# Attention and a token MLP on one core: half of the query projections moved into the attention loop, the second half's outputs moved behind it

## The chip, the core and the metric

The kernel runs on one core of a Trainium2 chip. The core has TensorE (PE in the profile, with PEld for its weight loads), VectorE (DVE), ScalarE (ACT), GpSimd (POOL) and SyncE (SP), which here issues nearly all transfers. The engines run their own instruction streams in order and wait for one another through semaphores. The metric is the device time of one execution in microseconds (us), as the median of several runs. The kernel before takes 1286.77 us, the median of 3 runs from 1286.64 to 1287.14.

## The reference

The input x has 2048 rows (tokens) and 512 columns. Two results are mixed by a gate of each row:

```python
x = A_x
g = _sigmoid((x * gate_w).sum(-1, keepdims=True))
a = _A_ref(x, A_wqkv, A_wo)           # softmax attention, 32 heads of 16 columns, then @ wo
b = _B_ref(x, B_w1, B_b1, B_w2, B_b2) # layernorm, then over the tokens: w1 (2048 x 1792), gelu, w2 (1792 x 2048)
return g * a + (1 - g) * b
```

In `_A_ref`, qkv = x @ wqkv, scores = q k^T / 4 for each head, p = softmax(scores), o = p v, and the result is o @ wo. All is in float32.

## The kernel before, in words

**Splitting.** Where float32 accuracy is wanted, a matrix is split into a part `hi`, rounded to the short form fp32r that PE multiplies at full speed, and the rest `lo`; a product is then three: hi x hi, hi x lo, lo x hi (`split` L64, `products` L69). A 128-column block of a product with 512 inner elements is so 4 x 3 = 12 matmuls of 128x512.

**Stages.** (1) x is loaded in 16 tiles of 128 rows, transposed on PE into `xt_hi`, `xt_lo` (L185 to L194), and v = x wv is put out by `v_out` (L221) into one SBUF tile `v`, with a column of ones beside each head, which later gives the softmax's sums. (2) The q/k stage (L362 to L387): for each block b of 128 columns (8 heads), four pieces of 512 tokens of k and four of q, each through `project` (12 matmuls into one of eight PSUM banks) and `parts` (L352: ACT casts hi, DVE subtracts lo, for queries ACT also makes |q| times the greatest |k|, a third plane; SP stores the planes `pc`, of which there are three buffers, to `kp_d` and `qp_d` in device memory). `greatest` keeps the largest |k| and |q|; from these `bring_most` and `least_shifts` set a flag that chooses the general path after the end, which these inputs do not take. (3) Layer one of the MLP (L449 to L475) with its gelu into `u_hi`, `u_lo`. (4) The attention loop, with layer two beside it. (5) The end, from L986.

**The attention loop.** There are 2 halves of the queries (1024 each) x 16 pairs of heads = 32 groups, each with 4 phases: 128 phases. `load_k` and `load_q` (L510, L515) fetch the next group's stacks from device memory: three planes of keys and four of queries for each of the two heads. Four rows of a stack's 64 x 2 are no data but -1 or the third plane, whose product shifts the exponent; the -1 rows of keys are set once by a POOL memset (`shift_rows` L491). In a phase, PE makes 16 scores of 128x512 (L917), ACT takes the exponential of 12 straight from PSUM, DVE copies the other four to SBUF (L934) for one ACT instruction of 2048 columns (L949), and `apply_v` (L792) makes 64 small products with v, whose sum DVE adds to `ot` (L821).

**Dense products beside the scores.** A score has only 64 inner rows, so it uses half of PE's rows; the other half takes half of a *dense* matmul at the same time (L926). A dense matmul is so done in two phases, its upper 64 rows in the one, its lower 64 in the next. Two phases are a *slot*, and there are 64 slots with at most 14 dense matmuls. The dictionary `dense` says what each slot holds, `calls` what is issued at a phase's start (transfers above all), `later` what DVE does at its end. They all sum into one PSUM bank, `dn`, and the slot's last step reads it out. Before, the first 28 matmuls of layer two are done at full width ahead of the loop (`first`, L831 to L837); slots 0 to 45 hold the rest of layer two (16 tiles of 42 matmuls), 46 and 47 nothing, 48 to 55 the output projections of the first half's eight token tiles (12 matmuls each), 56 to 63 the first 6 or 9 of the 12 of the second half's. The attention result is divided by its sums when it is fetched back from device memory (`fetch_half`, `fetch_o`, `load_wq`), into SBUF places of layer two, which is over by then (`open_end`).

**The end.** `others` (L995) makes the products that are left of the second half's eight output tiles, `last_pair` those with the last pair of heads, whose sums are only just known, and `finish` adds them to the MLP's share and stores them.

**What sets the order.** In stages 2 and 3 a scheduler orders the instructions of each engine; in the loop and at the end (`tc.manual_schedule`) they stand in the order of the code. Pools with `reuse_waits` make a new tile wait for the last reader of the old one.

## Time and profile before

| what | value |
|---|---|
| median of 3 runs | 1286.77 us |
| profiled execution | 1287.07 us, of which the span of instructions is 1284.9 us |
| PE / ACT / DVE / POOL busy | 1272.5 / 1087.6 / 670.8 / 199.1 us |
| mean granted clock of TensorE | 0.998 |
| stage 1 to first q/k product | 0 to 57.5 us |
| q/k stage, layer one | to 144.6, to 296.7 us |
| attention loop: first score, last product with v | 304.6, 1265.4 us |
| last product of the end | 1277.7 us |

A matmul's row in the trace gives its duration through the pipeline (0.39 us for 128x512), while the next begins 0.23 us after it; so PE's rate is read from starts, not from durations. In the chain of waits each row is a piece of work and the time that passed with it. Stretches are given as from:to, then length, then busy time and (x) count for PE, PEld, DVE, ACT and POOL, then granted clock, share of the transfer engines and GB/s. In rows of instructions the first number is the start, the second the time to the end of the group.

### The profile page before, as it was taken

The numbers are of one execution on the slowest core, as the hardware profiler recorded it, in microseconds if no ns is written. First come the engines' busy times: TensorE is split into PE (matmuls) and PEld (weight loads), VectorE is DVE, ScalarE is ACT, GpSimd is POOL, SyncE is SP. The second block draws the span as 40 slices with busy tenths as digits, with TensorE's granted clock in tenths as the row PEclk, the third lists the DMA queues.
The fourth block names the chain that finished last, engine by engine and source line by source line (L and its number), as shares of the span: only waits on it lengthen the run. The fifth ranks groups of instructions, "written<-read, shape, count | busy, mean of one in ns | idle before, by whom it ended". The sixth has DMA issues, their size and how long they took to land.

```text
span 1284.9 us, 33049 instructions
## 1 busy us (share of the span) xinstructions
PE 1272.5 (99%) x13281; PEld 837.1 (65%) x13281; DVE 670.8 (52%) x1138; ACT 1087.6 (85%) x1537; POOL 199.1 (15%) x306
## 2 busy tenths in 40 slices
PE   9999999999999999999999999999999999999997
PEld 7888888886666666666666666666666565655554
DVE  5675362537444544544444444444444675645555
ACT  3443343437999999999999999999999999999994
POOL 0210244455111111111111111111110000000000
PEclk9999999999999999999999999999999999999999
DMA  4496643327343344343334434433433754344412
GB/s 132 140 319 270 230 124 99 95 78 164 67 88 76 68 90 85 71 80 81 77 61 91 84 67 84 81 75 59 82 64 60 174 140 115 82 91 102 81 38 80
DMA packets 93581, 133.19 MB, mean 104 GB/s; under 512 B 16277, under 2 KB 55339, under 8 KB 90348
## 3 DMA queue, kind: packets, MB, share of 16 engines
q1 hardware_dynamic: 92844, 129.94, 41.8%
q8 instruction: 107, 1.75, 0.6%
q10 hardware_dynamic: 576, 1.05, 0.2%
q14 instruction: 54, 0.44, 0.1%
HBM read 97.00 MB, written 33.93 MB: 102 GB/s over the span
## 4 chain that ended last, share of the span: by engine, by line
PE 94%; ACT 4%; issue 1%; DVE 0%; DMA 0%; SPq 0%; ACTq 0%
PE av L799 29%; PE s L917 23%; PE t L917 12%; PE acc L417 12%; PE acc L74 10%; PE s L799 5%; PE dn L926 2%; ACT p L879 1%; ACT p L938 1%; ACT pe L949 1%; PE pa L1000 1%; PE dn L835 1%; PE acc L188 1%; PE acc L255 0%; PE pa L1030 0%
## 5 line engine op out<-in xcount | busy, mean ns | idle before, releaser
L938 ACT ACTIVATE p<-s 128x512 f32<-128x512 f32 x768 | 416.9, 817 | 1.5 <-PE s L917 1.5
L879 ACT ACTIVATE p<-t 128x1024 f32<-128x1024 f32 x352 | 370.5, 1300 | 0.0
L917 PE MATMUL s<-qs,ks 64*128 64x512 f32 x1344 | 342.0, 403 | 0.2
L934 DVE COPY pe<-s 128x512 f32<-128x512 f32 x512 | 318.0, 684 | 6.3 <-PE s L917 5.8
L917 PEld LDWEIGHTS s<-qs,ks 64*128 64x128 f32 x1344 | 234.7, 184 | 99.7 <-issue 52.2
L821 DVE TENSOR_TENSOR ot<-av,ot 128x512 f32<-128x512 f32 (+2 forms) x137 | 83.5, 610 | 393.3 <-PE av L799 393.0
L799 PE MATMUL av<-p,v 128*32 128x256 f32 x4904 | 288.1, 379 | 0.0
L949 ACT ACTIVATE pe<-pe 128x2048 f32<-128x2048 f32 x129 | 280.9, 2181 | 0.0
L799 PEld LDWEIGHTS av<-p,v 128*32 128x32 f32 x4904 | 159.3, 110 | 105.3 <-issue 0.2
L917 PE MATMUL t<-qs,ks 64*128 64x512 f32 x704 | 179.9, 450 | 1.7
L926 PE MATMUL dn<-u_hi,w_lo 64*128 64x512 f32 x430 | 174.8, 407 | 0.0
L926 PE MATMUL dn<-u_lo,w_hi 64*128 64x512 f32 x430 | 174.8, 406 | 0.0
L926 PE MATMUL dn<-u_hi,w_hi 64*128 64x512 f32 x428 | 173.5, 405 | 0.0
L67 POOL TENSOR_TENSOR w_lo<-w_raw,w_hi 128x512 fp32r<-128x512 f32 (+1 forms) x126 | 149.3, 1191 | 124.6 <-ACT w_hi L66 108.1
L917 PEld LDWEIGHTS t<-qs,ks 64*128 64x128 f32 x704 | 87.8, 184 | 90.0 <-ACT p L938 89.8
L930 POOL MEMSET token<- 1x1 f32 x124 | 12.3, 100 | 822.7 <-PE dn L926 757.4
L799 PE MATMUL av<-pe,v 128*32 128x256 f32 x2048 | 137.2, 385 | 0.1
L66 ACT CAST w_hi<-w_raw 128x512 fp32r<-128x512 f32 (+1 forms) x67 | 38.1, 569 | 79.4 <-PE acc L417 58.8
L799 PEld LDWEIGHTS av<-pe,v 128*32 128x32 f32 x2048 | 53.4, 109 | 54.8 <-ACT p L938 32.2
L417 PE MATMUL acc<-h_hi,w_hi 128*128 128x512 f32 x224 | 87.1, 389 | 0.0
L417 PE MATMUL acc<-h_lo,w_hi 128*128 128x512 f32 x224 | 87.1, 389 | 0.0
L417 PE MATMUL acc<-h_hi,w_lo 128*128 128x512 f32 x224 | 87.1, 389 | 0.0
(150 smaller groups left out, 1517.4 us busy)
## 6 DMA issues: line engine op xcount, KB each, us to landing
w_raw<-in_B_w_dram SPq DMA_DIRECT2D x96, 256.0 KB
ks<-kp SPq DMA_DIRECT2D x192, 128.0 KB
qs<-qp SPq DMA_DIRECT2D x256, 64.0 KB
qp<-pc SPq DMA_DIRECT2D x16, 768.0 KB
x<-in_A_x_dram SPq DMA_DIRECT2D x32, 256.0 KB
kp<-pc SPq DMA_DIRECT2D x16, 512.0 KB
w_raw<-in_B_w_dram SPq DMA_DIRECT2D x32, 128.0 KB
bp<-row SPq DMA_DIRECT2D x16, 256.0 KB
```

Of the source, the lines that this page charges most:

```text
L66: copy(hi, src)
L67: return sub(lo, src, hi.bitcast(F32), ALU.subtract)
L74: nc.tensor.matmul(ps, a, b, start=start and n == 0, stop=stop and n == last)
L417: nc.tensor.matmul(p, a, b, start=first and k == 0, stop=last and k == 2)
L799: mm = nc.tensor.matmul(av[32 * j : 32 * (j + 1), i * QC : (i + 1) * QC], v_flat[:, v_at : v_at + 32], pt[:, h * QC : (h + 1) * QC], start ...
L821: nc.vector.tensor_tensor(x, y, x, ALU.add)
L879: nc.scalar.activation(pt, twos[low, low + 1], AF.Exp, scale=SCALE)
L917: nc.tensor.matmul(s, kt[grp][rows_i, c * P : (c + 1) * P], qt[grp][rows_i, qb * NB : (qb + 1) * NB], start=True, stop=True,)
L926: mm = nc.tensor.matmul(ps, a[half], b[half], start=begin and not second, stop=last and bool(second))
L934: nc.vector.tensor_copy(pt, s)
L938: nc.scalar.activation(pt, s, AF.Exp, scale=SCALE)
L949: nc.scalar.activation(x, x, AF.Exp, scale=SCALE)
```

## The change: what it does

The q/k stage projects all four pieces of k but only the first two of q in each block (`jobs`). The other two of each block, eight pieces of 12 matmuls, become dense slots of the attention loop (`late_query`): after each of layer two's first eight tiles comes one such slot. For that the second half of transposed x is stored to device memory (`xt_d`, four transfers of 1 MB during block 0) and loaded again in two steps (`load_xt`), and the query weights are stored and loaded for each slot (`wq_d`). A slot's result goes through five DVE operations and three stores into `qp_d[1]`, which the second half's groups read. The bound check moves with it, from layer one into the loop.

Layer two then starts in slot 0 and nothing is done at full width ahead of the loop. Slots 0 to 31 hold eight tiles of layer two and the eight query pieces, 32 to 55 the other eight tiles, 56 to 63 the outputs of the first half. All 96 matmuls of the second half's outputs stand in the end.

v is four tiles, one for each block of eight heads. When a block's last group is over, its place takes fetched rows of the first half (`fetch_left`), later others. v itself is first stored to device memory for the general path.

The first place is PE between layer one (`acc`) and the first scores (`s`, from the stacks `qs`, `ks`). Before:

```order
L417 MATMUL acc<-h_lo,w_hi 128x512
L417 MATMUL acc<-h_hi,w_lo 128x512
L835 MATMUL dn<-u_hi,w_hi 128x512
L835 MATMUL dn<-u_lo,w_hi 128x512
L835 MATMUL dn<-u_hi,w_lo 128x512
```

and, 23 rows of L835 further on,

```order
L835 MATMUL dn<-u_hi,w_hi 128x512
L917 MATMUL s_2818<-qs,ks_2703 128x512
L926 MATMUL dn<-u_lo,w_hi 128x512
L917 MATMUL s_2819<-qs,ks_2703 128x512
L926 MATMUL dn<-u_hi,w_lo 128x512
```

Now, at the same place:

```order
L417 MATMUL acc<-h_lo,w_hi 128x512
L417 MATMUL acc<-h_hi,w_lo 128x512
L982 MATMUL s_2692<-qs,ks_2619 128x512
L991 MATMUL dn<-u_hi,w_hi 128x512
L982 MATMUL s_2693<-qs,ks_2619 128x512
L991 MATMUL dn<-u_lo,w_hi 128x512
L982 MATMUL s_2691<-qs,ks_2619 128x512
L991 MATMUL dn<-u_hi,w_lo 128x512
```

The 28 full-width products are gone, and the first score follows layer one's last product. On POOL the memset of the first keys' shift rows stands, before and now, behind the same last weight split; before:

```order
L67 TENSOR_TENSOR w_lo<-w_raw,w_hi 128x512 x3
L493 MEMSET ks_2703 16x2048 x2
L930 MEMSET token 1x1
L493 MEMSET ks_2704 16x2048 x2
```

and now:

```order
L67 TENSOR_TENSOR w_lo<-w_raw,w_hi 128x512 x3
L489 MEMSET ks_2619 16x2048 x2
L995 MEMSET token 1x1
L489 MEMSET ks_2620 16x2048 x2
```

Nothing moved there. The second place is DVE at the end of slot 3 (the fourth phase of the second group): `pe` are the copied scores, `dn` the dense bank, `row` a buffer of 128x512, `z` the greatest values. Before:

```order
L934 COPY pe<-s_3645 128x512
L934 COPY pe<-s_3676 128x512
L523 TENSOR_SCALAR row<-dn,b2x_75,omg 128x512
L66 CAST w_hi<-w_raw 128x512
L821 TENSOR_TENSOR ot<-av,ot 128x512
```

Now:

```order
L999 COPY pe<-s_3515 128x512
L999 COPY pe<-s_3546 128x512
L66 CAST row<-dn 128x512
L67 TENSOR_TENSOR row<-dn,row 128x512
L564 TENSOR_SCALAR row<-dn,most 128x512
L565 SCALAR_TENSOR_TENSOR row<-row 128x512
L566 TENSOR_REDUCE z<-dn 128x1
L894 TENSOR_TENSOR ot<-av,ot 128x512
```

Five operations stand now between the last copy and the addition to `ot`, four of which read `dn`. The third place is SP's queue at the change from stage 1 to the q/k stage. Before:

```order
L173 DMA x<-in_A_x_dram 128x512 x3
L159 DMA wc_raw<-in_A_wqkv_dram 128x4x128 x2
L135 DMA w_raw<-in_B_w_dram 128x512 x4
```

with two more of each of the last two kinds, and then the first `kp` store. Now:

```order
L400 DMA xt_68<-xt_hi 512x1x512
L183 DMA x<-in_A_x_dram 128x512
L400 DMA xt_69<-xt_lo 512x1x512
L183 DMA x<-in_A_x_dram 128x512
L169 DMA wc_raw<-in_A_wqkv_dram 128x4x128 x2
L145 DMA w_raw<-in_B_w_dram 128x512 x2
L397 DMA wq_72<-wc_hi 128x512
L169 DMA wc_raw<-in_A_wqkv_dram 128x4x128
L400 DMA xt_70<-xt_hi 512x1x512
L400 DMA xt_71<-xt_lo 512x1x512
L397 DMA wq_73<-wc_lo 128x512
```

The four stores of transposed x and the first query weights (`wq`) have come in ahead of the first key store. The diff, cut to its core:

```diff
-    qp_d = [dram.tile([3, P, S], F32, name=f"qp{b}") for b in range(ND)]
+    qp_d = [[dram.tile([3, P, S // 2], F32, name=f"qp{h}{b}") for b in range(ND)] for h in range(2)]
+    xt_d = {n: [dram.tile([P, ND, NB], F32, name=f"xt{n}{i}") for i in range(2)] for n in (2, 3)}
+    wq_d = [[dram.tile([P, ND, P], F32, name=f"wq{b}{i}") for i in range(2)] for b in range(ND)]
+    v_d = [dram.tile([P, NS * (P // DH) * VC], F32, name=f"v{b}") for b in range(ND)]
...
-    v_pool = ctx.enter_context(tc.tile_pool(name="v", bufs=1))
-    v_flat = v_pool.tile([P, NS * H * VC + HALF], F32, name="v")
-    v = v_flat[:, : NS * H * VC].rearrange("p (t h c) -> p t h c", h=H, c=VC)
+    v_pool = ctx.enter_context(tc.tile_pool(name="v", bufs=1, reuse_waits="tile"))
+    BH = P // DH
+    BV = NS * BH * VC
+    def v_tile(b, dtype):
+        return v_pool.tile([P, BV + DH], dtype, name=f"v{b}")
+    vb = [v_tile(b, F32) for b in range(ND)]
+    v = [x[:, :BV].rearrange("p (t h c) -> p t h c", h=BH, c=VC) for x in vb]
...
-            nc.scalar.copy(v[:, t, :, 0:DH], ps.rearrange("p (h d) -> p h d", d=DH))
+            heads = ps.rearrange("p (b h d) -> p b h d", h=BH, d=DH)
+            for b in range(ND):
+                nc.scalar.copy(v[b][:, t, :, 0:DH], heads[:, b])
...
+        jobs = [(n, True) for n in range(NQ)] + [(n, False) for n in range(NQ // 2)]
         for b in range(ND):
             wk_b, wq_b = qk_w.pop(0), qk_w.pop(0)
             kmax = bd.tile([P, NQ], F32, name="kmax")
-            qmax = bd.tile([P, NQ], F32, name="qmax")
-            for n in range(NQ):
-                ps = project(wk_b, n)
-                parts(ps, kp_d[b], n)
-                greatest(kmax[:, n : n + 1], ps)
-            nc.vector.tensor_reduce(kmax[:, 0:1], kmax, axis=AX.X, op=ALU.max)
-            nc.vector.tensor_scalar_mul(kmax[:, 0:1], kmax[:, 0:1], BOUND_SLACK)
-            for n in range(NQ):
-                ps = project(wq_b, n)
-                parts(ps, qp_d[b], n, kmax[:, 0:1])
-                greatest(qmax[:, n : n + 1], ps)
-                if n % 2 and qk_cols:
+            for at, (n, keys) in enumerate(jobs):
+                ps = project(wk_b if keys else wq_b, n)
+                if keys:
+                    parts(ps, kp_d[b], n)
+                    greatest(kmax[:, n : n + 1], ps)
+                else:
+                    parts(ps, qp_d[0][b], n, most[:, b : b + 1])
+                    greatest(qmax[:, b, n : n + 1], ps)
+                if n == NQ - 1:
+                    nc.vector.tensor_reduce(kmax[:, 0:1], kmax, axis=AX.X, op=ALU.max)
+                    nc.vector.tensor_scalar_mul(most[:, b : b + 1], kmax[:, 0:1], BOUND_SLACK)
+                if at in (1, 4) and qk_cols:
                     qk_w.append(wcols(qk_cols.pop(0)))
-                if n % 2 == 0:
-                    c = 2 * b + n // 2
+                if at in (2, 5):
+                    c = 2 * b + at // 3
                     ln_load(ln, c)
                     ln_rows(ln, c)
-                if b == ND - 1:
+                if at in (3, 4):
+                    nc.sync.dma_start(wq_d[b][at - 3], wq_b[at - 3].bitcast(F32))
+                if b == 0 and keys:
+                    src = (xt_hi, xt_lo)[n % 2][:, :, (2 + n // 2) * NB : (3 + n // 2) * NB]
+                    nc.sync.dma_start(xt_d[2 + n // 2][n % 2], src.bitcast(F32))
+                if b == ND - 1 and at > 1:
                     load_weight()
-                    if n > 0:
+                    if at > 2:
                         split_weight()
-            nc.vector.tensor_reduce(qmax[:, 0:1], qmax, axis=AX.X, op=ALU.max)
-            nc.vector.tensor_mul(most[:, b : b + 1], qmax[:, 0:1], kmax[:, 0:1])
...
-                    if f0 == 0 and c == 0:
-                        bring_most()
-                    if f0 == 0 and c == NH + 4:
-                        least_shifts()
...
+    def load_xt(n):
+        xt[n] = [o_pool.tile([P, ND, NB], F32R, name=f"big{i}") for i in range(2)]
+        for dst, src in zip(xt[n], xt_d[n]):
+            nc.sync.dma_start(dst.bitcast(F32), src)
...
+    def late_query(b, n):
+        box = []
+        def load():
+            for i in range(2):
+                t = out_pool.tile([P, D], F32, name="row", bufs=3)
+                nc.sync.dma_start(t.rearrange("p (k c) -> p k c", k=ND), wq_d[b][i])
+                box.append(t.bitcast(F32R).rearrange("p (k c) -> p k c", k=ND))
+        def out():
+            ps, cols = box[2], slice((n - 2) * NB, (n - 1) * NB)
+            hi, lo, most_k = (out_pool.tile([P, D], F32, name="row", bufs=3) for _ in range(3))
+            split(hi.bitcast(F32R), lo.bitcast(F32R), ps, nc.vector.tensor_copy, nc.vector.tensor_tensor)
+            nc.vector.tensor_scalar(most_k, ps, most[:, b : b + 1], None, ALU.mult)
+            nc.vector.scalar_tensor_tensor(most_k.bitcast(F32R), most_k, -1.0, most_k, ALU.mult, ALU.max)
+            nc.vector.tensor_reduce(qmax[:, b, n : n + 1], ps, axis=AX.X, op=ALU.max, apply_absolute_value=True)
+            for i, t in enumerate((hi, lo, most_k)):
+                nc.sync.dma_start(qp_d[1][b][i, :, cols], t)
+        def step(k, j):
+            first, last = k == j == 0, k == ND - 1 and j == 2
+            if first:
+                box.append(ps_dn.tile([P, D], F32, name="dn"))
+            a, x = ((0, 0), (0, 1), (1, 0))[j]
+            return box[2], box[a][:, k, :], xt[n][x][:, k, :], first, last, out if last else None
+        return [(step, k, j) for k in range(ND) for j in range(3)], load
...
+    def v_block(b):
+        if b not in in_place_of_v:
+            in_place_of_v[b] = v_tile(b, F32R)[:, : NS * P].rearrange("p (t x) -> p t x", x=P)
+        return in_place_of_v[b]
...
+    def fetch_left(k, *ats):
+        first = 8 * (k % 2)
+        parts = [v_block(k // 2)[:, at : at + 4] for at in (first, first + 4)]
+        fetch(0, k, left, parts, out_pool.tile([P, NB], F32, name="row", bufs=3), ats)
+    def fetch_right(k, *ats):
+        both = pieces(place(k))
+        fetch(0, k, right, (both[:, :4], both[:, 4:]), end.tile([P, QW], F32, name="o_sum", bufs=3)[:, :NB], ats)
...
-    for k in range(ND):
-        call(6 * k + 5, load_wo, k, 6 * k + 5)
-    steps = second_layer(0)
-    first, at = steps[:28], put(steps[28:], 0, [14])
-    for t in range(1, NS):
+    call(1, load_xt, 2)
+    for b in range(ND):
+        call(6 + b, nc.sync.dma_start, v_d[b], vb[b][:, :BV])
+    at, queries = 0, [(b, n) for n in (2, 3) for b in range(ND)]
+    for t in range(NS):
         at = put(second_layer(t), at, [14] * 3)
+        if queries:
+            b, n = queries.pop(0)
+            at = put_whole(late_query(b, n), at)
+            if (b, n) == (ND - 1, 2):
+                call(2 * at, load_xt, 3)
+            if (b, n) == (ND - 1, 3):
+                call(2 * at, open_wo)
+                on_dve(2 * at + 1, greatest_of_all)
+                call(2 * at + 2, bring_most)
+                on_dve(2 * at + 4, least_shifts)
+                for k in range(ND):
+                    call(2 * at + 5 + 4 * k, load_wo, k, 2 * at + 5 + 4 * k)
...
+    left, right = slice(0, NB), slice(NB, QW)
+    for k in range(ND):
+        p0 = PHASES * (NP + 4 * (k // 2 + 1)) + 3 + 4 * (k % 2)
+        assert p0 + 3 < 2 * at
+        call(p0, fetch_left, k, p0 + 2, p0 + 2, p0 + 2)
...
-        call(p0 + k // 2, fetch_half, k, left, p0 + 2 + k // 2, p0 + 2 + k // 2)
-        call(p0 + 2 + k // 2, fetch_half, k, right, p0 + 5 + k, p0 + 5 + k)
-    at += 2
+        call(p0 + k, fetch_right, k, p0 + k + 2, p0 + k + 2, p0 + k + 2)
     for t in range(NH):
-        at = put_output(t, 3 * ND, at)
-    p1 = PHASES * (NP + 2 * 4) + 3
-    call(p1, fetch_o, 1, 0, (8, 9), (p1 + 2, p1 + 3, p1 + 3))
-    call(p1 + 4, fetch_o, 1, 1, (10, 11), (p1 + 6, p1 + 7, p1 + 7))
-    p2 = PHASES * (NP + 3 * 4) + 3
-    assert p2 >= 2 * at - 1
-    call(p2, fetch_o, 1, 2, (0, 1), (p2 + 1, p2 + 1, p2 + 2))
-    call(p2 + 4, load_wq, p2 + 4)
-    call(LAST - 1, fetch_o, 1, 3, (2, 3), (LAST, LAST, LAST), 3)
-    for t in range(NH, NS):
-        at = put_output(t, 6 if 2 * at < p2 + 3 else 9, at)
-    assert at == NG * PHASES // 2
+        at = put_whole(project(t), at)
+        call(p0 + 2 * t, load_base, NH + t)
+    assert p0 + 7 < 2 * (at - 4) and at == NG * PHASES // 2
+    call(p0 + 4, fetch_o, 0, p0 + 6, p0 + 6, p0 + 7)
+    call(p0 + 6, fetch_o, 1, p0 + 8, p0 + 8, p0 + 10)
+    call(p0 + 7, load_wq, p0 + 7)
+    call(p0 + 9, fetch_o, 2, p0 + 11, p0 + 12, p0 + 12)
+    call(LAST - 1, lambda: fetch_o(3, LAST, LAST, LAST, pairs=3))
...
-        for n, (step, *args) in enumerate(first):
-            if n and n % 12 == 0:
-                split_weight(nc.vector.tensor_copy, nc.vector.tensor_tensor)
-            ps, a, b, start, stop, done = step(*args)
-            nc.tensor.matmul(ps, a, b, start=start, stop=stop)
-            if done:
-                done()
...
-        LATE = 3, 5, 7
+        LATE = 3, 5, 6, 7
         def others(*tiles, m=0, n=3 * ND):
             for t in tiles:
-                mms = list(enumerate(o_matmuls(1, NH + t, early[NH + t], 3 * ND)))
+                mms = list(enumerate(o_matmuls(1, NH + t, 0, 3 * ND)))
...
-        others(2, 4, 6)
+        others(2, 4)
...
-        last_pair(0, parts)
-        others(1)
+        last_pair(0, parts, LATE)
+        others(6, 1)
...
-        others(*LATE)
+        others(3, 5, 7)
```

143 lines of the change are left out of this document (75 added, 68 removed).

## The prediction

> **What bounds the kernel now.** I read the page first (span, busy shares, slices, chain), then the chain of waits in order of time, then stretches with the busy time of each engine, and last single instructions at the places that the change touches.
>
> ```profile
> span 1284.9 us, 33049 instructions
> PE   9999999999999999999999999999999999999997
> ACT  3443343437999999999999999999999999999994
> PE 94%; ACT 4%; issue 1%; DVE 0%; DMA 0%; SPq 0%; ACTq 0%
> ```
>
> TensorE (PE) is busy throughout, and ScalarE (ACT) from the tenth slice (about 300 us) to the last but one. So there are two regimes: PE alone before 300 us, both of them in the attention loop. The chain gives the stretches:
>
> ```profile
> 52.04 92.54 PE acc L74 x408
> 144.58 149.39 PE acc L417 x660
> 298.05 6.63 PE dn L835 x28
> 945.40 3.65 PE av L799 x64
> 975.39 3.65 PE av L799 x64
> 1035.34 3.65 PE av L799 x64
> 1065.34 3.64 PE av L799 x64
> ```
>
> The 408 products of L74 (24 of the last two v tiles, then 32 x 12 = 384 of the q and k projections) run without a gap at 92.54 / 408 = 0.2268 us each. Layer one follows, then the 28 products of `first`, then attention. The last four rows stand at the same place of four groups: 945.40 to 975.39 is a group whose slots hold 14 dense products (30.0 us), 975.39 to 1035.34 two groups, one of them with two empty slots (59.95, so 29.97 each), 1035.34 to 1065.34 a group with 12 (30.0). A phase takes 7.49 us whatever rides beside its scores. Why:
>
> ```profile
> 975.00:1005.00 30.00, 29.90 (x352) 16.62 (x350) 13.75 (x22) 30.00 (x43) 0.80 (x4) 1.00 0.41 94
> 1035.00:1065.00 30.00, 29.82 (x370) 18.06 (x370) 22.20 (x39) 30.00 (x43) 0.88 (x5) 1.00 0.51 125
> 985.15 2.19 ACT L949 ACTIVATE pe<-pe 128x2048 f32<-128x2048 f32 x1
> 992.62 2.20 ACT L949 ACTIVATE pe<-pe 128x2048 f32<-128x2048 f32 x1
> ```
>
> Columns of the first two rows are PE, weight loads, DVE, ACT, POOL, clock, DMA share, GB/s. ACT is busy 30.00 of 30.00 with and without dense products, and its exponentials return every 7.47 us also in empty slots. The attention loop belongs to ACT; products of 12 to 14 per slot are free there as long as nothing else waits on them.
>
> **The change part by part.** The sum is made against the profiled execution, 1287.07 us (span 1284.9 and 2.2 around it); the median of the runs shown is 0.30 lower, 1286.77.
>
> *Fewer projections ahead.* Two of four query pieces in each of four blocks leave the q/k stage: 2 x 4 x 12 = 96 products x 0.2268 = **-21.8 us**, if PE still sets the pace. With them go 8 ACT casts, 8 ACT multiples, 8 DVE subtractions and 8 reductions, all beside PE. What is added there are transfers on SP's queue: four of 1 MB (transposed x) and eight of 0.26 MB (query weights), while eight of 0.79 MB go.
>
> ```profile
> 57.50:144.60 87.10, 87.10 (x386) 72.13 (x385) 56.16 (x111) 36.93 (x63) 6.90 (x5) 1.00 0.71 260
> 65.00:110.00 45.00, 45.00 (x201) 37.24 (x200) 31.98 (x59) 21.17 (x37) 5.60 (x4) 1.00 0.89 317
> 60.00:65.00 5.00, 5.00 (x24) 4.14 (x23) 3.57 (x15) 2.78 (x5) 0.00 (x0) 1.00 0.07 27
> ```
>
> Two of the 1 MB stores stand between the last loads of x, two before the first key store, where the transfers rest (27 GB/s from 60 to 65). After that stand 16 x 0.52 (keys) + 8 x 0.79 (queries) + 8 x 0.26 (x) + 6 x 0.26 (query weights) + 3 x 0.26 (projection weights) + 4 x 0.26 (layer-one weights) = 20.2 MB. The stage would last 24 x 12 x 0.2268 = 65.3 us, to 122.8. At the 317 GB/s that were kept up for 45 us, 20.2 MB take 64 us; begun at about 62 they end near 126, 3 us behind PE. PE does not see this: eight banks and three `pc` buffers lie between a product and its store. Cost taken: 0.
>
> *v's blocks.* A v tile is put out by four ACT copies and no longer one, ahead of the next transpose's cast on ACT.
>
> ```profile
> L222 ACT COPY v<-acc 128x512 f32<-128x512 f32 x16 | 9.3, 588 | 26.6 <-PE acc L74 26.1 <-PE acc L255 0.6
> 285.87 0.41 ACT L66 CAST w_hi<-w_raw 128x256 fp32r<-128x256 f32 x1 [0.43 <-POOL w_lo L67]
> 40.41 0.69 DVE L67 TENSOR_TENSOR xt_lo<-acc,xt_hi 128x512 fp32r<-128x512 f32 x1 [1.64 <-ACT xt_hi L66]
> 42.15 0.49 PE L74 MATMUL acc<-wv_hi,xt_hi 128*128 128x512 f32 x1
> ```
>
> A 512-wide copy takes 0.59 us, a 256-wide cast 0.41, so a 128-wide one about 0.3 (estimate by the same slope), four of them 0.6 more. The transposed tile was whole at 41.10 in the tightest turn and read at 42.15: 1.05 us of cover. Cost 0; if the cover goes, 14 turns x 0.1 to 0.3 us.
>
> *No `first` products.* They took 298.05 to 304.60. Their removal does not give 6.6 us, since the first score waits for other things too:
>
> ```profile
> 296.51 0.39 PE L417 MATMUL acc<-h_hi,w_lo 128*128 128x512 f32 x1
> 296.30 5.17 SPq L508 DMA_DIRECT2D qs<-qp  x8
> 298.49 1.75 POOL L67 TENSOR_TENSOR w_lo<-w_raw,w_hi 128x512 fp32r<-128x512 f32 x1 [0.78 <-ACT w_hi L66]
> 300.30 3.87 POOL L493 MEMSET ks<- 16x2048 f32 x2
> 304.60 0.49 PE L917 MATMUL s<-qs,ks 64*128 64x512 f32 x1
> ```
>
> The two memsets of the keys' shift rows end at 304.17, behind the same last weight split on POOL, which the change leaves in place; the eight query loads are issued until 301.47. So the first score moves from 304.60 to about 304.3, seen from the end of layer one: **-0.3 us**. (Bounds: 0, and -1.1 if the memset is not what is awaited and only the loads are.)
>
> And PE now stands idle there, from 296.7 to 304.3. What an idle PE does to its clock is shown at the end of this trace, and what a cold PE does at its start:
>
> ```profile
> 1277.30 0.39 PE L1000 MATMUL pa<-wo_hi,e 96*128 96x512 f32 x1
> 1280.00:1280.50 0.50, 0.00 (x0) 0.00 (x0) 0.00 (x0) 0.00 (x0) 0.00 (x0) 1.00 0.28 98
> 1281.00:1281.50 0.50, 0.00 (x0) 0.00 (x0) 0.00 (x0) 0.00 (x0) 0.00 (x0) 0.50 0.00 0
> 1.21 2.74 PE L232 MATMUL acc<-idle 128*128 128x512 bf16 x6 [1.21 <-DVE idle L227]
> 4.33 0.59 PE L232 MATMUL acc<-idle 128*128 128x512 bf16 x2
> ```
>
> After the last product (ended 1277.7) the granted clock is 1.00 until 1280.5 and 0.50 from 1281.0: about 3 us of idleness halve it, and the gap is 7.6 us. At the start six 512-wide products take 2.74 us, about 0.45 each, and from 4.33 two take 0.59, the later pitch: about 3.1 us of work until full speed. So phase 0 loses half of 3.1 = 1.55 us of PE work. ACT hides some: first score to first score of the next phase is 304.60 to 311.42 = 6.8 us on PE against ACT's 7.49, so 0.7 is cover, and 0.9 to 1.55 are lost. I take **+1.3 us**, near the upper end because the first exponential itself starts later. Bounds: 0, and 3.4 if all 6.8 us of phase 0 run at half speed. This speaks against the change. The Trainium skill, TensorE: Matmul & The Clock Gate, section "What's actually happening", says that a whole idle window of about 3.4 us halves the clock and a busy one restores it, with free-running windows; a gap of 7.6 us always holds a whole window. The rows agree on both times; by the page's transition at around 4 us the loss would be 2.0, the sum 0.7 us higher.
>
> *Query slots.* Eight slots of 12 products stand in the attention loop; by the rows above they cost ACT nothing. Five DVE operations follow each instead of none, and all but one read the only `dn` bank, which the next slot's first product needs. A slot with the same place in its group:
>
> ```profile
> 1047.24 2.48 DVE L934 COPY pe<-s 128x512 f32<-128x512 f32 x4
> 1049.64 0.74 DVE L676 SCALAR_TENSOR_TENSOR row<-dn,g,row 128x512 f32<-128x512 f32 x1
> 1053.90 0.50 PE L926 MATMUL dn<-wo_hi,e 64*128 64x512 f32 x1
> 1054.03 0.69 DVE L821 TENSOR_TENSOR ot<-av,ot 128x512 f32<-128x512 f32 x1 [1.17 <-PE av L799]
> L67 DVE TENSOR_TENSOR h_lo<-hf,h_hi 128x512 fp32r<-128x512 f32 x16 | 16.4, 1026 | 9.9 <-ACT h_hi L66 9.9
> ```
>
> DVE is free for the bank from 1049.64, and the next product on it starts at 1053.90: 4.26 us. Four copies in 2.48 are 0.62 each; five such operations are 3.1 to 3.5 us. Cover of 0.75 us or more remains. Cost 0; with the longest mean of a 512-wide operation (1026 ns) they would be 5.1 us, 0.9 over, eight times. The loads for a slot (two weight pieces; x itself in two pairs of 1 MB) are issued two or more phases ahead. Each slot's three stores wait on SP for the DVE results, and behind them stand the next query and key loads, which have two phases (15 us) until they are read. The four stores of v (1.1 MB each), the bound check with its two small transfers and the four loads of wo only change place in the loop, where the DMA share is 0.41 to 0.51 and DVE 14 to 22 of 30 us busy; cost 0.
>
> *Outputs.* The eight output tiles of the first half take slots that were there. Of the second half's 96 products, before, 3 x 6 + 5 x 9 = 63 were done in slots; now all stand behind the last score.
>
> ```profile
> 1267.18 3.44 PE pa L1000 x15
> 1275.42 0.91 PE pa L1000 x3
> 1276.35 2.12 DVE base L1043 x3
> ```
>
> PE is the chain through this tail and nothing else delays it: 63 x 3.44/15 = **+14.4 us**. The end after the last product is four transfers close together before (DVE to 1278.47, transfers to about 1280.5) and one alone now: **-0.3 us** (bounds 0 and -0.8). The first half's fetched rows, placed in v's used blocks, only shift 12 DVE operations of 0.7 us into phases with 4 us of room.
>
> **Sum:** -21.8 - 0.3 + 1.3 + 14.4 - 0.3 = -6.7 us: 1280.4 against the profiled execution, **1280.1 us** against the median (-0.5%).
>
> **The rivals.**
> *No cold start.* If PE's clock survives the gap, or ACT hides the whole of it, the 1.3 us go: 1278.8. For it: ACT sets the loop's pace. Against: its first exponential waits on PE.
> *The bank held too long.* If the five DVE operations last over 4.26 us, PE waits at eight slots and ACT runs dry. At 0.9 us over, 8 x 0.9 = 7.2: 1287.3, within the bound of no change. For it: L67's 1026 ns while POOL works on the same data; against: PSUM readers in the loop at 0.62.
> *Transfers bind the q/k stage (slower).* Four banks and three `pc` buffers are all that is left when layer one asks for its banks: 7 x 12 x 0.2268 = 19 us of lag. At rate r the stores end near 62 + 20.2 MB/r; at 260 GB/s that is 139.7, 17 us late and still hidden; at 220 it is 153.8, 31 late, 12 us uncovered: 1292. It makes the kernel slower than before from about 225 GB/s down (9.3 us uncovered). For it: the queue is 0.89 busy over 45 us already and gets 4 MB at its start. Against: 317 GB/s kept up there; 260 is a mean that includes the pauses.
> *The change does not do what it says* (the 96 products are not in the way, or the tail hides its new ones) is excluded: both are gapless PE stretches on the chain.
>
> **How the numbers follow.** Forecast with its terms 0.60; no cold start 0.16; bank or other small waits in the loop that eat most of the gain 0.10; slower, by the transfers or another wait of over 9 us, 0.12; better than all these 0.02. Runs of before differ by 0.04%, so 0.2% (2.6 us) is about what can be told. Under 1284.2 lie the forecast, no cold start, the better case and a third of the waits: faster 0.81; the rest of the waits is the same, 0.07; slower 0.12. Range: low 1277.8 (no cold start, -1.1 at the start, -0.8 at the end would be 1277.5), high 1285.5 (cold phase 0 throughout, +2.1, and 0.4 us at each query slot); it leaves out the slower case and some of the third.
>
> **What would show it.** The stretch of L74 products should shrink from 92.5 to 70.8 us without a gap; the time between layer one's last product and the first score should be 7.5 to 8 us, with a clock of 0.5 in the first 3 us of scores; groups of four phases should stay at 30.0, also those with a query slot at their end; the tail from the last av to the last product should grow by 14.4. A gap on PE before layer one, or a group of 31 us or more, would make the prediction wrong.

## The result

The changed kernel takes 1280.48 us (median of 5 runs, 1279.80 to 1281.11); the kernel before, run beside it, 1286.77 (1286.50 to 1287.42). The ratio is 0.995 with a 95% interval of 0.9935 to 0.9965, which leaves out no change: faster by 6.3 us. The profiled execution took 1280.37 us, 6.70 less than that of before, of which 6.5 are span.

From the page of the changed kernel, its span and two slice rows:

```profile
span 1278.4 us, 33281 instructions
PE   9999999989999999999999999999999999999998
ACT  4443344269999999999999999999999999999990
```

The two regimes are as before. ACT's own runs from the ninth slice now, and PE has a slice with an 8 in it: the gap ahead of attention. The chain in order of time (start, us, engine, tile, line, count) gives the stretches:

```profile
51.74 70.78 PE acc L74 x312
122.52 151.74 PE acc L417 x660
274.70 3.76 DMA ks<-kp
278.48 4.82 DMA qs<-qp
746.04 3.66 PE av L872 x64
776.02 3.66 PE av L872 x64
806.00 3.66 PE av L872 x64
1247.84 7.66 PE pa L1065 x33
1257.09 5.78 PE pa L1065 x24
1264.47 8.59 PE pa L1065 x36
```

What the reader is to see: the q/k stage fell from 92.54 to 70.78 us without a gap; layer one, which the change does not touch, grew from 149.39 to 151.74; two transfers stand on the chain ahead of attention; groups still take 30.0 us, also where a query slot (the one at 761) lies between; and the last three rows hold 93 of the tail's 96 full products. The instructions around the first score (start, us, engine, line, operation, and in brackets the idle time before it and what ended it):

```profile
276.81 0.39 PE L417 MATMUL acc<-h_hi,w_lo 128*128 128x512 f32 x1
276.58 9.87 SPq L504 DMA_DIRECT2D qs<-qp  x16
280.57 3.82 POOL L489 MEMSET ks<- 16x2048 f32 x2
283.30 0.76 PE L982 MATMUL s<-qs,ks 64*128 64x512 f32 x1 [6.09 <-DMA qs<-qp]
291.46 0.50 PE L982 MATMUL s<-qs,ks 64*128 64x512 f32 x1 [0.22 <-ACT p L944]
```

The gap from layer one's last product to the first score is 6.49 us (before: 296.51 to 304.60, 8.09), and phase 0 lasts 8.16 us (before 6.82). The whole difference of the spans, place by place:

| place | before | after | difference |
|---|---|---|---|
| start to the q/k stage | 52.04 | 51.74 | -0.3 |
| q/k stage | 92.54 | 70.78 | -21.8 |
| layer one's pace | 149.39 | 151.74 | +2.35 |
| its last product to the first score | 8.09 | 6.49 | -1.6 |
| first score to the tail's first product | 960.76 | 962.72 | +2.0 |
| tail, first to last product | 12.33 | 27.02 | +14.7 |
| last product to the end | 7.21 | 5.36 | -1.85 |

The rows add up to -6.5. (Layer one's last product is counted from its start, the tail's to its end; 2.55 us of layer one, the same in both kernels, stand in no row. The first row is within scatter: the q/k stage's row starts between 51.7 and 52.7 in the changed kernel and its variants, at 52.0 and 51.9 in the two profiles of before.) The predicted total was nearly the measured one, but three rows are not those of the prediction: layer one, the gap, and the end. The experiments go after these and after the costs taken as zero. Each is the changed kernel with one edit, unless said otherwise. A number like "-1.7 us" is its median's distance to the kernel before on the same chip, less the -6.29 of the changed kernel.

### The profile page after: what moved, and what is told of

It is laid out like the page before. It is cut to its first block, busy times and chain, and to the rows that moved or that the text cites. A ratio compares the mean times of both kernels' runs of the same rounds, so it can differ in the third digit from the quotient of the medians.

```text
span 1278.4 us, 33281 instructions
## 1 busy us (share of the span) xinstructions
PE 1262.8 (99%) x13342; PEld 835.1 (65%) x13342; DVE 684.0 (54%) x1149; ACT 1081.4 (85%) x1569; POOL 201.8 (16%) x318
## 3 DMA queue, kind: packets, MB, share of 16 engines
q8 instruction: 108, 1.77, 0.6%
## 4 chain that ended last, share of the span: by engine, by line
PE 97%; ACT 1%; DMA 1%; issue 0%; DVE 0%; SPq 0%; ACTq 0%
PE av L872 30%; PE s L982 24%; PE acc L417 12%; PE t L982 12%; PE acc L74 8%; PE s L872 5%; PE dn L991 3%; PE pa L1065 2%; ACT p L944 1%; PE acc L198 1%; PE acc L267 0%; DMA qs<-qp 0%; ACT p L1003 0%; DMA ks<-kp 0%; ACT pe L1014 0%
## 5 line engine op out<-in xcount | busy, mean ns | idle before, releaser
L982 PE MATMUL s<-qs,ks 64*128 64x512 f32 x1344 | 345.5, 401 | 6.7 <-DMA qs<-qp 6.1
L982 PEld LDWEIGHTS s<-qs,ks 64*128 64x128 f32 x1344 | 239.3, 185 | 101.5 <-issue 51.9
L991 PE MATMUL dn<-u_hi,w_hi 64*128 64x512 f32 x448 | 183.4, 409 | 0.0
L991 PE MATMUL dn<-u_lo,w_hi 64*128 64x512 f32 x448 | 182.6, 408 | 0.0
L991 PE MATMUL dn<-u_hi,w_lo 64*128 64x512 f32 x448 | 181.8, 406 | 0.0
L67 POOL TENSOR_TENSOR w_lo<-w_raw,w_hi 128x512 fp32r<-128x512 f32 (+1 forms) x128 | 152.9, 1200 | 121.9 <-ACT w_hi L66 100.6
L417 PE MATMUL acc<-h_hi,w_hi 128*128 128x512 f32 x224 | 87.9, 392 | 0.0
L417 PE MATMUL acc<-h_hi,w_lo 128*128 128x512 f32 x224 | 87.8, 392 | 0.0
L417 PE MATMUL acc<-h_lo,w_hi 128*128 128x512 f32 x224 | 87.8, 392 | 0.0
```

The lines of the kernel that those rows point to most:

```text
L67: return sub(lo, src, hi.bitcast(F32), ALU.subtract)
L417: nc.tensor.matmul(p, a, b, start=first and k == 0, stop=last and k == 2)
L982: nc.tensor.matmul(s, kt[grp][rows_i, c * P : (c + 1) * P], qt[grp][rows_i, qb * NB : (qb + 1) * NB], start=True, stop=True,)
L991: mm = nc.tensor.matmul(ps, a[half], b[half], start=begin and not second, stop=last and bool(second))
```

## The experiments

### Layer one: where the second h tile lies

In layer one the first products of rows c = 0 to 7 come at the old pace and those of c = 8 to 15 do not; stretches of 20 us of the changed kernel, with L417's own instructions (PE busy and count, weight loads, clock, DMA share, GB/s):

```profile
124.00:144.00 20.00, 20.00 (x90) 16.57 (x89) 1.00 0.70 223
146.00:166.00 20.00, 20.00 (x87) 16.10 (x86) 1.00 0.35 104
```

The clock is 1.00 in both, and the slower stretch has fewer transfers beside it. The change took four small tiles out of pool `bd`, and the tiles that hold rows 8 to 15 are allocated behind it: the hi part at byte 88064 of each partition in the program before, at 85792 now, the lo part 16384 bytes further on. First a pad of 64 for 56 elements, in both kernels.

```diff
-    bd.tile([P, 56], F32, name="pad", bufs=1)
+    bd.tile([P, 64], F32, name="pad", bufs=1)
```

> The changed kernel with the unused pad tile of pool bd 64 instead of 56 elements wide: the second h tile (rows of c = 8 to 15) moves from byte 85792 to byte 85824 of each partition, from 32 past a multiple of 64 to a multiple of 64. Nothing else moves. Theory (the place of the moving operand sets the pitch): the products of c = 8 to 15 go back from 0.2337 to 0.2267 us, layer one from 151.74 to 149.4 us, the time from 1280.5 to 1278.1. Rival (the slower pitch comes from transfers or other engines at work in that stretch): layer one stays at 151.7 and the time at 1280.5.

> The same edit on the kernel before: there it moves the second h tile from byte 88064 (a multiple of 64) to 88096 (32 past one). Theory (place): layer one grows from 149.39 to 151.7 us and the time from 1286.8 to 1289.1, with nothing of the change in the kernel. Rival (transfers, or something else of the change): layer one stays at 149.4, the time at 1286.8.

Measured: in the changed kernel 1278.88 (1278.59 to 1279.58), -1.7 us; in the kernel before 1289.27 (1288.78 to 1290.13, 11 runs), 2.4 us slower than without the edit, ratio 1.002 (1.0011 to 1.0029). Layer one in the first, then in the second:

```profile
123.11 150.32 PE acc L417 x659
```
```profile
144.44 151.74 PE acc L417 x660
```

The kernel before turns as slow as the changed one by 32 bytes alone. That settles the cause: no transfer, no wait, but the place. In the other direction the mend is only partial: at byte 85824, 64 past a multiple of 128, layer one is between the two. So a coarser boundary counts:

```diff
-    bd.tile([P, 56], F32, name="pad", bufs=1)
+    bd.tile([P, 112], F32, name="pad", bufs=1)
```

> The changed kernel with the pad tile of pool bd 112 instead of 56 elements wide: the second h tile moves from byte 85792 to 86016, a multiple of 256 (with 64 elements it lay 64 past a multiple of 128 and its products took 0.2289 us, at 32 past a multiple of 64 they took 0.2336). If the pitch is full speed only from a coarser boundary than 64, all of layer one runs at 0.2267: 149.4 us, the time 1278.1. If 64 bytes were all that counts, layer one stays at the 150.3 us of the run with 64 elements: 1278.9.

Measured: 1278.11 (1277.37 to 1278.53), ratio to before 0.993 (0.9917 to 0.9944), -2.6 us. The chain and the second stretch of 20 us:

```profile
123.19 149.39 PE acc L417 x660
```
```profile
146.60:166.60 20.00, 20.00 (x90) 16.56 (x89) 1.00 0.35 105
```

Full pace, 90 products in 20 us again.

### The gap: cold clock and first score

The clock in the changed kernel's stretches of 1 us (PE, weight loads, DVE, ACT, POOL, clock, DMA share, GB/s):

```profile
280.00:281.00 1.00, 0.00 (x0) 0.00 (x0) 0.97 (x2) 0.06 (x1) 0.94 (x2) 0.76 0.95 135
281.00:282.00 1.00, 0.00 (x0) 0.00 (x0) 1.00 (x2) 0.44 (x1) 1.00 (x1) 0.50 1.12 160
287.00:288.00 1.00, 1.00 (x10) 1.00 (x8) 0.69 (x1) 0.74 (x2) 0.00 (x0) 0.83 0.30 93
```

It is 0.50 from 280.52 (0.76 in that microsecond) to 287.34 (0.83 in its own), and PE works at half speed from the first score at 283.30 on, for 4.0 us. To price this, PE was kept at work through the gap:

```diff
+        with tc.manual_schedule(engines={mybir.EngineType.PE}):
+            kept = bank()
+            for _ in range(26):
+                nc.tensor.matmul(kept, u_hi[:, 0, :P], u_hi[:, 0, :], start=True, stop=True)
     h_ctx.close()
```

> The changed kernel with 26 unneeded products (one u block by itself, into a bank that nobody reads) in the gap between layer one and the first score: 26 x 0.2267 = 5.9 of its 6.5 us, so PE is never idle for over 1 us there. By the prediction's term for the cold clock the time falls by 1.3 us, to 1279.2; by what the two traces show between the first score and phase 2 (1.71 us) to 1278.8; by the rival 'no cold start' it stays at 1280.5. In the trace the clock should be 1.00 in the first scores and phase 0 last 6.8 us instead of 8.16.

Measured: 1278.76 (1278.47 to 1279.28), -1.8 us. From the second on, the first scores stand 0.23 us apart, not 0.43:

```profile
283.41 0.47 PE L986 MATMUL s<-qs,ks 64*128 64x512 f32 x1
283.72 0.39 PE L986 MATMUL s<-qs,ks 64*128 64x512 f32 x1
283.95 0.39 PE L986 MATMUL s<-qs,ks 64*128 64x512 f32 x1
```

So the cold clock costs 1.7 to 1.8 us of the 2.0 that PE loses in 4.0 us at half speed; ACT hides little of it. The rival without a cold start is out. Next the start part alone, undone with real products:

```diff
+        steps = second_layer(t)
+        if t == 0:
+            first, at = steps[:28], put(steps[28:], 0, [14]) + 2
...
+        for n, (step, *args) in enumerate(first):
+            if n and n % 12 == 0:
+                split_weight(nc.vector.tensor_copy, nc.vector.tensor_tensor)
```

> The changed kernel with the 28 products of the first second-layer tile put back between layer one and the first score, as before; the two slots that they fill in the changed kernel (slots 1 and 2) stay empty, all else keeps its slot. This undoes the start part alone. By the prediction's terms (-0.3 for the gap, +1.3 for the cold clock) the part costs 1.0, so the time falls to 1279.5. By the two traces (-1.6 for the gap, +1.7 for the clock) it is worth nothing: 1280.4. If there were no cold start, the time rises by 1.6, to 1282.1.

Measured: 1281.46 (1280.60 to 1281.51), +0.9 us: none of the three, since the edit brought a wait of its own. The gap is 8.07 us and the clock 1.00, as before the change, but phase 0 lasts 7.36 us, not 6.82:

```profile
285.69 0.43 DVE L66 CAST w_hi<-w_raw 128x512 fp32r<-128x512 f32 x1 [0.69 <-DMA w_raw<-in_B_w_dram]
287.57 0.50 PE L994 MATMUL s<-qs,ks 64*128 64x512 f32 x1 [0.44 <-DVE pe L1011]
```

DVE waits for a weight that is still under way, its copies of scores come late, and PE waits for them. Less 0.5 us for that, the start part is about even or a slight gain, which fits the traces (-1.6 and +1.7) and not the loss of 1.0 that was predicted. With half as many products:

```diff
-            first, at = steps[:28], put(steps[28:], 0, [14]) + 2
+            first, at = steps[:14], put(steps[14:], 0, [14] * 2) + 1
```

> The changed kernel with 14 (not 28) products of the first second-layer tile ahead of the first score; slot 2 stays empty. They run from about 278.5 to 281.7, inside the gap, with about 1.5 us of idleness on either side. If 3 us of idleness are what halves the clock, the clock stays at 1.00 and the first score does not move: 1278.8, as with the 26 unneeded products. If it was not the 28 products' length that cost the run with all of them 1.0 us, but the weights that they use up early, phase 0 waits for a weight again: 1279.3 or more.

Measured: 1279.54 (1279.11 to 1279.98), -1.0 us. The clock stays at 1.00 and the first score is not delayed (283.07), but phase 0 waits for DVE's copies again, behind a weight split that DVE does at 282.52 and 284.29. Almost half of the warm clock's gain is lost to that, about as the second expectation had it, though DVE is here kept by the split and layer one's gelu and not by a load that is late.

What the first score waits for was tried by issuing every second one of the first group's query loads from ACT:

```diff
-                landed.append(nc.sync.dma_start(dst[at].bitcast(F32), src[b][part[which], rows, :]))
+                landed.append(queues[n % len(queues)].dma_start(dst[at].bitcast(F32), src[b][part[which], rows, :]))
...
+        stack(t, qp_d[half], 0, pair, [*PAIRS, SHIFT], (nc.sync, nc.scalar) if g == 0 else (nc.sync,))
```

> The changed kernel with every second one of the first group's eight query loads issued by ACT's queue instead of SP's, so the fourth, on which the first score waited, is issued at about 277.3 instead of 278.5. If the first score waits for that load, it comes about 1.1 us earlier (5.4 us behind layer one), until the first memset (ended 282.5) binds: 1279.4, with the clock still cold. If it waits for the memsets of the keys' shift rows, as the prediction had it, nothing moves: 1280.5.

```profile
279.41 3.99 POOL L489 MEMSET ks<- 16x2048 f32 x2
282.59 0.76 PE L982 MATMUL s<-qs,ks 64*128 64x512 f32 x1 [5.28 <-DMA qs<-qp]
```

The first score comes 0.8 us sooner behind layer one than in the changed kernel's profile (5.28 us of idleness, not 6.09) and again starts before the second memset's end at 283.40: of the memsets it waits for the first only. But the 0.8 us can't be put down to the edit. In four runs that leave the gap's code alone (the pads of 64 and 112, and the two of the next section) PE stood idle for 5.39 to 5.41 us, and the score started within 0.1 us of the first memset's end. In the run of the next section with longer DVE work:

```profile
280.92 3.82 POOL L489 MEMSET ks<- 16x2048 f32 x2
282.94 0.79 PE L983 MATMUL s<-qs,ks 64*128 64x512 f32 x1 [5.39 <-POOL ks L489]
```

So either the first memset or the query loads come last, by up to 0.7 us, and the changed kernel's profile shows an execution with late loads. The time, 1279.86 (1279.03 to 1280.25), is 0.6 to 0.8 us lower, but its runs overlap those of the changed kernel, so a gain is not shown.

### The query slots and the queue: how much cover there was

The slot that ends at 340.5, in the changed kernel:

```profile
340.56 0.68 DVE L66 CAST row<-dn 128x512 fp32r<-128x512 f32 x1
343.27 0.68 DVE L566 TENSOR_REDUCE z<-dn 128x1 f32<-128x512 f32 x1
344.82 0.50 PE L991 MATMUL dn<-u_hi,w_hi 64*128 64x512 f32 x1
```

DVE is done with the bank at 343.95, 3.4 us after it began, and 0.87 us remain until the next product on it (0.85 to 0.87 in all eight slots). To see whether that cover is real:

```diff
-            nc.vector.tensor_reduce(qmax[:, b, n : n + 1], ps, axis=AX.X, op=ALU.max, apply_absolute_value=True)
+            for _ in range(4):
+                nc.vector.tensor_reduce(qmax[:, b, n : n + 1], ps, axis=AX.X, op=ALU.max, apply_absolute_value=True)
```

> The changed kernel with three more reductions of the same bank behind each of the eight query tiles (the fifth operation repeated): DVE reads the bank for 3.4 + 3 x 0.61 = 5.2 us instead of 3.4, against the 4.26 us until the next product on it. If every us over counts (the price of the rival 'bank held too long'), 8 x 1.0 us are lost: 1288. If scores that do not need the bank and the buffers of ACT cover it, less than 2 us: 1280.5 to 1282.5.

Measured: 1291.29 (1290.69 to 1291.87), +10.6 us, slower than before the change (ratio 1.0033, 1.0021 to 1.0045). The same slot, and the waits of PE from 280 to 800 us (us in total, times, longest):

```profile
340.45 0.68 DVE L66 CAST row<-dn 128x512 fp32r<-128x512 f32 x1
343.16 2.86 DVE L567 TENSOR_REDUCE z<-dn 128x1 f32<-128x512 f32 x4
PE dn L992 <- DVE z L567: 7.8, 8, 1.0
```

DVE holds the bank for 5.57 us, since the three reductions take 0.73 each and not 0.61; that is 1.31 us more than the 4.26 there are. The loss is 1.3 us a slot: nothing covers it, and every us over counts, as the rival had it. (PE's wait is listed with 1.0, since it is counted from the modelled end of the product before it.) This rival's mechanism is real; the change stays clear of it by 0.87 us a slot.

The queue in the q/k stage, with 8 MB more to store:

```diff
                     nc.sync.dma_start(xt_d[2 + n // 2][n % 2], src.bitcast(F32))
+                    for m in range(2):
+                        nc.sync.dma_start(more_d[2 + n // 2, n % 2, m], src.bitcast(F32))
```

> The changed kernel with each of the four 1 MB stores of transposed x made three times, into DRAM that nobody reads: 8 MB more in the queue at the head of the q/k stage. By the prediction's count (28.2 MB from 62 us, at the 345 GB/s that the changed kernel kept up from 70 to 100 us) the stores end near 144, 21 us behind PE, of which 19 are hidden: 2 us lost at most, 1282.5. At the mean rate of 260 GB/s they would end at 170, with 29 us uncovered: 1309. If nothing hid the lag, 21 us: 1301.

Measured: 1294.18 (1293.61 to 1294.85), +13.5 us, and not by any of the three counts. PE's wait, the load of the weights on SP's queue, ACT's last two rows before the wait ends, and a stretch with the clock:

```profile
PE acc L74 <- ACT wc_hi L66: 8.5, 1, 8.5
82.13 1.70 SPq L170 DMA_DIRECT2D wc_raw<-in_A_wqkv_dram  x1
92.52 0.58 ACT L66 CAST pc<-acc 128x512 fp32r<-128x512 f32 x1 [9.68 <-DMA qp<-pc]
93.26 0.62 ACT L66 CAST wc_hi<-wc_raw 128x512 fp32r<-128x512 f32 x1 [0.16 <-DMA wc_raw<-in_A_wqkv_dram]
90.00:100.00 10.00, 5.94 (x15) 4.28 (x16) 4.71 (x8) 3.25 (x6) 1.27 (x1) 0.55 1.03 367
```

What PE lacks, for its eleventh projection, is the weights, and two things hold them up that end within 1 us of one another. Their load is issued at 82.13, behind the stores, and lands just before 93.26. And ACT, which casts them, stands until 92.52 at the plane before them in its stream, which waits 9.68 us for a `pc` buffer that a late store still holds. The cold clock after the 8.5 us comes on top. In the changed kernel the same load, the fourth of its kind, stands ahead of the key stores, and the cast is done 16 us before PE reads it:

```profile
53.46 0.38 SPq L169 DMA_DIRECT2D wc_raw<-in_A_wqkv_dram  x1
67.98 0.62 ACT L66 CAST wc_hi<-wc_raw 128x512 fp32r<-128x512 f32 x1 [1.96 <-PE acc L74]
84.28 0.39 PE L74 MATMUL acc<-xt_hi,wc_hi 128*128 128x512 f32 x1
```

So the edit did more than add bytes: the scheduler also put this load behind the stores. That late transfers can stop PE here is shown; how many MB more the changed kernel would bear in its own order is not.

### The end

```diff
-        others(3, 5, 7)
+        others(3, 5, 7, n=9)
+        others(3, 5, 7, m=9)
```

> The changed kernel with the last three output tiles' products in another order: nine of each first, then three of each, so that, as before the change, three gated sums and four stores come close together behind the last products; the count of products is the same. If the end was shortened by the change because only one tile is left at the last product (5.36 us from it to the end of the span instead of 7.21), it grows back by 1.9: 1282.3. If the end has nothing to do with how close the stores stand, 1280.5.

```profile
1271.23 2.14 DVE L1108 SCALAR_TENSOR_TENSOR base<-pa,g,base 128x512 f32<-128x512 f32 x3 [6.40 <-PE pa L1065]
```

Measured: 1281.87 (1280.89 to 1282.36), +1.3 us, with the three gated sums back to back as before the change. So most of the 1.85 us at the end came from there being one tile left at the last product. The profiled execution shows 1.0 of it (6.3 us from the last product to the end); it is the fastest of the five, with the low clock for only 2.9 us behind the first score.

### Together

> The changed kernel with what the runs so far showed to pay, together: the h tile at a multiple of 256 (-2.4), 14 products ahead of the first score (-1.7), the first group's query loads on two queues (-0.6), and in the slot that the 14 leave free nine products of one of the second half's output tiles, which then has three behind the last score (-9 x 0.2293 = -2.1). If all add up: 1280.5 - 6.8 = 1273.7. If the gap's three parts share one price (a shorter gap is worth less when the clock is warm), up to 0.6 less.

> The changed kernel with the three small mends together and nothing else: the h tile at a multiple of 256 (-2.4 alone), unneeded products in the gap, 22 of them since the gap is shorter here (-1.7 alone), and the first group's query loads on two queues (-0.6 alone). No weight is used early and no slot changes. If they add, 1280.5 - 4.7 = 1275.8, with the first phase 6.8 us long. If the earlier loads are worth something only while the clock is cold, 1276.4.

The first of these changes, beside the three edits shown above (pad 112, 14 products ahead, two queues), the second half's output tile 3: `project` takes a number of products, nine of them stand in slot 63, and `others` begins at the tenth for that tile. Measured: 1275.77 (1275.38 to 1275.91), ratio to before 0.9914 (0.99 to 0.9927). It beats both kernels, by 11.1 and 4.8 us, but not by the sum of the parts. The missing 2.0 us are in phase 0, which lasts 9.1 us: its first score comes early, at 280.24, yet its waits are

```profile
283.43 0.50 PE L997 MATMUL s<-qs,ks 64*128 64x512 f32 x1 [1.31 <-ACT p L1018]
284.42 0.50 PE L997 MATMUL s<-qs,ks 64*128 64x512 f32 x1 [0.49 <-DVE pe L1014]
```

ACT and DVE still finish layer one's gelu and a weight split then. What bounds the start of attention, once PE is warm and its loads are early, is those two.

The second, 22 idle products with the pad and the two queues, took 1277.24 (1276.69 to 1279.03): -3.8 us of the -4.7 expected, and it scatters over 2.3 us. The profiled execution is its slowest one. Its first score comes 7.3 us behind layer one's last product (6.5 in the changed kernel's profile), since it waits for query loads; and the clock was cold although PE stood idle for 1.92 us only:

```profile
282.71 0.47 PE L986 MATMUL s<-qs,ks 64*128 64x512 f32 x1 [1.92 <-DMA qs<-qp]
283.00:284.00 1.00, 1.00 (x8) 1.00 (x8) 1.00 (x2) 0.69 (x2) 0.00 (x0) 0.63 0.56 152
286.00:287.00 1.00, 1.00 (x9) 1.00 (x7) 0.69 (x1) 0.74 (x3) 0.00 (x0) 0.67 1.46 370
```

The clock falls at 283.26, after PE has taken up work again, and returns at 286.66. That its faster runs stayed warm is argued from their times and their mean clocks (0.999 to 1.000, against 0.998); they have no profile.

## Why the prediction came out as it did

*Fewer projections ahead* (-21.8): right, 21.76 measured, gapless. The transfers' zero was right as well. But the lag of 19 us, counted from banks and buffers alone, was not the nearest cover: ACT casts the planes and the projection weights in one stream, so a store that holds a `pc` buffer holds the next weights too, and these are cast 14 to 16 us before PE reads them. The slower rival was therefore closer than its 31 us of lag made it; how close stays open.

*Layer one* had no term, and that is the step that failed: the prediction counted the instructions that the change moves, and took a stage with the same instructions to last as long. It lasted 2.35 us longer, because tiles removed from the pool ahead of it moved an operand by 2272 bytes. The runs with the pad, in both kernels, show it.

*No first products* (-0.3): mis-sized, -1.6 measured in the profiled execution, -2.3 in the four runs with the same gap where the loads were not late. The prediction had the first score wait for both memsets. The score reads the upper half of the rows only, so it needs one of them and four query loads; it started 1.1 us before the second memset ended. Even the lower bound of -1.1 was short of it.

*Cold clock* (+1.3): right in kind, 1.7 to 1.8 measured. The prediction took 3.1 us of work at half speed; it was 4.0. The Trainium skill, TensorE: Matmul & The Clock Gate, section "What's actually happening", gives a free-running window of 3413 ns. The trace agrees: 280.52 to 287.34 is 6.82 us, two windows, and how much of them lies behind the first score differs from run to run (2.9 us with the last stores close together, 6.2 with the pad of 112). By that page's transition, at about 4 us, the prediction had put 2.0; the measurement lies between.

*v's blocks* (0): right, within the scatter of the q/k stage's start (0.3 us earlier here).

*Query slots* (0): right, with numbers as forecast: 3.4 us of DVE work (3.1 to 3.5 predicted) and 0.87 us of cover left (0.75 or more). The longer edit bears out the rival's price: 1.3 us over, 1.3 us lost, at each of eight slots.

*Outputs* (+14.4): right within 0.3. The tail's full products came every 0.2325 us or so, against 0.2293 in the row that the term was taken from; why was not tried. *The end* (-0.3): mis-sized, -1.85 measured, 1.3 of it given back when the last stores stand close again. The bound of -0.8 was too narrow; what of the 1.85 lies in the stores and what behind them was not taken apart.

The total was close by luck, because these errors cancel in the profiled execution: +2.35 in layer one, +0.4 cold clock, +0.3 tail and +0.25 in the rest of the loop, against -1.3 for the gap, -1.55 for the end and -0.3 at the start.

## What to carry to other kernels

When a change removes or adds tiles, list the addresses of all that is allocated behind them: a stage whose instructions did not change can change its pace, and a pad of a few bytes mends it. When a stage's cover is computed, look for everything that shares its queue or the stream of the engine that handles it, loads ahead of all, since the nearest deadline decides and not the longest buffer. When PE is left waiting, a few idle products are cheaper than real ones that use up operands early.

## What the runs showed of the hardware

A product of 128 x 512 fp32r (stationary 128 columns) took 0.2267 us with its moving operand at a multiple of 256 bytes in the partition (tiles at 52736, 86016 and, before, 88064), 0.2290 at 64 past a multiple of 128 (85824), and 0.2334 at 32 past a multiple of 64 (85792, and 88096 in the kernel before). Whether 128 past a multiple of 256 is at full pace was not tried, nor the place of the stationary operand.

The clock's low stretches come in lengths of one or two times 3.41 us: 6.82 in the changed kernel, 3.41 in the run with 22 idle products. The changed kernel's full clock before the gap, from 4.04 to 280.52, is 81 times that. So windows of 3.41 us can be counted from the clock's first rise, and PE's idle time in each can be read. First two windows of the run with the query loads on two queues, then two of the run with 22 idle products (first column of work PE; the clock stands behind POOL):

```profile
275.65:279.06 3.41, 1.66 (x8) 1.04 (x6) 3.37 (x4) 2.40 (x4) 3.34 (x3) 1.00 1.09 239
279.06:282.47 3.41, 0.00 (x0) 0.00 (x0) 3.34 (x5) 0.68 (x2) 3.30 (x3) 1.00 0.84 142
279.84:283.25 3.41, 1.49 (x9) 1.02 (x9) 3.19 (x6) 1.87 (x4) 2.05 (x2) 1.00 0.58 132
283.25:286.67 3.42, 3.42 (x20) 3.42 (x18) 3.06 (x5) 2.56 (x5) 0.00 (x0) 0.50 0.69 195
```

With 1.75 us of idleness in a window the clock stays for the next one; with 1.92 it falls, though PE works in all of the next. The 14 profiled executions agree: at full clock no window with 1.77 us or less was followed by the low clock, and each with 1.92 or more was. At the low clock a window with 0.48 us of idleness brought it back (the run with the last stores close together), one with 0.61 did not (the pad of 112). So what counts in these traces is the idle share of a window, from a little over half on, and not the length of a gap: "about 3 us of idleness", as the prediction read it, is not a safe bound.
